# Staging the first MLP weight matrix in five slots instead of three, two of them in the x^T buffer

## The chip, the cores and the metric

One core of one Trainium2 chip runs the kernel. The metric is the device time of one execution in microseconds (us). TensorE, VectorE, ScalarE, GpSimd (POOL) and SyncE each run their own list of instructions in order and wait for one another through semaphores. DMA transfers are issued by SyncE, ScalarE or POOL.

## The reference

With x of 2048 rows (S) and 512 columns (D), the result mixes two branches by a gate per row, `out = g * a + (1 - g) * b`:

```python
g = sigmoid((x * gate_w).sum(-1, keepdims=True))
# a: 32 heads of 16; row s looks at the 8 rows s, s-2, ..., s-14
a = softmax(q . k * 16**-0.5, over the 8 rows) . v  @ wo        # q, k, v = x @ wqkv
# b: an MLP over the rows (tokens), not over the columns
h = layernorm(x)
u = gelu(einsum("bsd,sf->bdf", h, w1) + b1)      # F = 1792
b = transpose(einsum("bdf,fs->bds", u, w2) + b2)
```

W1 is 2048 x 1792 and W2 is 1792 x 2048, both bf16, 7.3 MB each, so neither is held on the chip whole.

## The kernel before

**Stages.** All on-chip buffers are views of one array, `arena`. TensorE's work is one fixed chain of steps: transposes of the first four tiles of x, the projections to q, k and v (L645), the first MLP product `u^T = W1^T h` (L853, called ph2), the second MLP product (L880, ph3) with the attention's output projection added into the same bank (L889), and the final scaling to the output. VectorE computes the attention: products of q and shifted k, sums, softmax pieces, and products with shifted v. TensorE's two short steps called sum0 and sum1 (L709 and L714), one for each half of the rows, sum the products over a head's 16 columns. They stand in TensorE's order inside ph2: sum0 inside block 1, sum1 after block 11. sum0 also computes the gate from x^T, and is the last reader of x^T.

**ph2.** It has 14 blocks (`ft` = 0 to 13), each of 16 matmuls of 128x128 weights by 128x512 data, one per tile of 128 rows. Blocks 2j and 2j+1 use load `w1_j`, which brings 256 columns of W1: 1 MB, as 16 x 256 elements for each of 128 partitions. There are three slots, and load j goes to slot j % 3:

```python
w1ld[j] = load("w1_%d" % j, W1W[:, j % 3, :, :], ..., ["w1s%d" % (j % 3)], order=j < 3)   # L529
```

So load j + 3 may start when block 2j + 1 has read its slot (L866 and L867). After each block ScalarE applies gelu and writes `UT[ft]`.

**ph3.** It has 16 tiles of 128 output rows, each of 14 matmuls in two halves of 7. Tiles 2j and 2j+1 use load `w2_j` (0.9 MB). The eight W2 slots (`W2S`, L368) lie on buffers no longer in use: two on x^T, three on the W1 slots, two on x, one on softmax scratch. The first six half tiles go in the order (0,0) (1,0) (2,0) (0,1) (1,1) (2,1) (L908). The output projection of tile i (`wo`, 4 matmuls) follows tile i + 5 (`LAG`); those of the last six stand at the very end, the last in two halves. It reads the attention's result `OT[i // 2]`, which VectorE writes.

**What sets the order.** A planner in the kernel (`_Sched`) lists every operation with what it reads and writes under names such as `w1s0` or `xt1`, derives the dependencies, and orders each engine's list by estimated times. An operation that writes a name waits for the last writer and all readers of that name. `after=` fixes only an order of issue, without a wait. W1 and W2 are loaded by SyncE, in the order `w1_0`, `w1_1`, `w1_2`, `wo`, `w1_3` to `w1_6`, `w2_0` to `w2_7`. SyncE holds a load until its semaphores are reached, and all loads behind it with it. `w1_1` and all later loads also wait for one accumulating copy of the attention (`late_dep`). The name list `XTALL` (L367) stands for all of x^T. A load with `XTALL` among its writes waits for sum0, and a second such load waits for the first to land.

**Other DMA.** POOL issues four copies of the softmax weights per half (L782, 512 KB each, on-chip to on-chip), which spread each head's weights over its columns for VectorE; they start when that half's softmax is done. For units 3, 4 and 5 of the v products POOL also issues accumulating copies (L822) which VectorE waits for before its next additions.

Of the kernel before, what the change touches and what calls it, by code (L numbers as in the profile page):

```python
# [5 lines left out]
BF16 = mybir.dt.bfloat16  # L6
# [6 lines left out]
S = 2048  # L13
# [5 lines left out]
NST = S // 128  # L19
NFT = F // 128  # L20
# [260 lines left out]
class _Mem:  # L281
# [17 lines left out]
    def view(self, name, dtype, dims, extra=0, p0=0, np_=128):  # L299
        base = self.arena[:].bitcast(dtype)  # L300
        pst = base.ap[0][0]
        esz = mybir.dt.size(dtype)
        o = self.off[name]
        assert o % esz == 0
        return bass.AP(base.tensor, p0 * pst + o // esz + extra, [[pst, np_]] + [list(d) for d in dims])


def bass_gated_mix__sliding_local_dilated__mixer_token_mlp__prompt_kernel(nc, A_x, A_wqkv, A_wo, B_x, B_w1, B_b1, B_w2, B_b2, gate_w, out, dbg=None):
    with contextlib.ExitStack() as es:
# [35 lines left out]
        view = m.view  # L345
        ps = es.enter_context(nc.psum_tensor("ps", [128, 8, 512], FP32))
# [7 lines left out]
        w1v = B_w1.rearrange("(st p) f -> p st f", p=128)  # L354
# [3 lines left out]
        X = view("X", BF16, [(D, NST), (1, D)])  # L358
        XT = view("XT", BF16, [(S, 4), (1, S)])
        UT = view("UT", BF16, [(D, NFT), (1, D)])  # L360
        WQKV = view("WQKV", BF16, [(3 * D, 4), (1, 3 * D)])
        W1W = view("W1", BF16, [(NST * 256, 3), (256, NST), (1, 256)])

        def w2view(name, extra=0):
            return view(name, BF16, [(256, NFT), (1, 256)], extra=extra)

        XTALL = ["xt0_%d_%d" % (t, k_) for t in range(4) for k_ in range(2)] + ["xt1", "xt2", "xt3"]  # L367
        W2S = [w2view("XT"), w2view("XT", NFT * 256), w2view("W1", NST * 256), w2view("W1", 2 * NST * 256), w2view("W1"),  # L368
               w2view("X"), w2view("X", NFT * 256), w2view("S4")]
        W2ALIAS = [XTALL, XTALL, ["w1s1"], ["w1s2"], ["w1s0"],  # L370
                   ["x%d" % t for t in range(7)], ["x%d" % t for t in range(7, 14)], ["s4", "s2", "s1", "rs", "rb"]]
        assert 4 * UT_ * 4 + 2 * UT_ * 4 + 2 * UT_ * 4 + UT_ * 2 >= NFT * 256 * 2
        WO = view("WO", BF16, [(D, 4), (1, D)])
# [57 lines left out]
        def col(v_, i):  # L431
            return bass.AP(v_.tensor, v_.offset + i, [list(v_.ap[0]), [1, 1]])
# [14 lines left out]
        def act(o_, i_, f_, **kw):  # L447
            return lambda e: e.activation(out=o_, in_=i_, func=f_, **kw)  # L448
# [29 lines left out]
        w1ld = {}  # L478
        late_dep = [[]]

        def load(name, dst, src, nbytes, writes, transpose=False, queue="sp", issue=0.5, order=True, deps=(), after=()):
            ds = sch.dsem(name)

            def fn(e):
                if transpose:
                    return e.dma_start_transpose(dst, src)
                return e.dma_start(dst, src)
            op = sch.dma(queue, fn, nbytes, ds, issue=issue, writes=writes, deps=list(deps) + late_dep[0],
                         after=list(after) + ([last_ld[queue]] if order and queue in last_ld else []), name=name)
            if order:  # L490
                last_ld[queue] = op
            return op
# [33 lines left out]
        ld_w("wv", 2, 0, 4, "wv")  # L526

        def ld_w1(j):
            w1ld[j] = load("w1_%d" % j, W1W[:, j % 3, :, :], w1v[:, :, 256 * j:256 * j + 256], S * 256 * 2, ["w1s%d" % (j % 3)], order=j < 3)  # L529

        def ld_w2(j):
            w1ld[7 + j] = load("w2_%d" % j, W2S[j], w2v[:, :, 256 * j:256 * j + 256], F * 256 * 2, ["w2_%d" % j] + W2ALIAS[j], order=False,
                               after=[w1ld[6 + j]])

        ld_w1(0)

        def f_warm(n):
# [9 lines left out]
        def PE(fn, dur, reads, writes, name, prio=0):  # L547
            op = A("pe", fn, dur, reads=reads, writes=writes, after=([chain[0]] if chain[0] is not None else []), name=name, prio=prio)
            chain[0] = op
            return op  # L550
# [234 lines left out]

        late_dep[0] = [qkd[0, 1]]
        ld_w1(1)
        ld_w1(2)
        load("wo", WO, A_wo.rearrange("(p t) d -> p t d", p=128, t=4), D * D * 2, ["wo"])

        def f_te(e):
            ins = None
            for k_ in range(4):
                ins = e.transpose(out=psb(3)[:, 128 * k_:128 * k_ + 128], in_=EB[:, 128 * k_:128 * k_ + 128], identity=IDENT)  # L794
            return ins
# [53 lines left out]
        def f_ph2(ft, bank, half):  # L849
            def fn(e):  # L850
                ins = None
                for st in range(8 * half, 8 * half + 8):
                    ins = e.matmul(ps[:, bank, :], lhsT=W1W[:, (ft // 2) % 3, st, 128 * (ft % 2):128 * (ft % 2) + 128], rhs=X[:, st, :],  # L853
                                   start=(st == 0), stop=(st == NST - 1))
                return ins
            return fn

        MLPB = [1, 2, 0, 1, 2, 0, 3, 1, 2, 0, 3, 1, 2, 0]
        for ft in range(NFT):
            bank = MLPB[ft]  # L860
            for half in range(2):
                PE(f_ph2(ft, bank, half), 1.735, ["x%d" % t for t in range(8 * half, 8 * half + 8)] + ["w1s%d" % ((ft // 2) % 3)], ["b%d" % bank],
                   "ph2_%d_%d" % (ft, half))
            A("act", act(UT[:, ft, :], ps[:, bank, :], AF.Gelu_apprx_tanh, bias=col(B1C, ft)), 0.7,
              reads=["b%d" % bank, "b1c"], writes=["ut%d" % ft] + (["wq0", "wq1", "wk", "wv"] if ft == 0 else []), name="gel%d" % ft, table=GELU)
            if ft % 2 == 1 and ft // 2 + 3 <= 6:  # L866
                ld_w1(ft // 2 + 3)  # L867
        for j in range(8):
            ld_w2(j)

# [5 lines left out]
        def f_ph3(i, bank, half, c0=0, c1=D):  # L876
            def fn(e):
                ins = None
                for ft in range(7 * half, 7 * half + 7):
                    ins = e.matmul(ps[:, bank, 0:c1 - c0], lhsT=W2S[i // 2][:, ft, 128 * (i % 2):128 * (i % 2) + 128], rhs=UT[:, ft, c0:c1],  # L880
                                   start=(ft == 0), stop=False)
# [27 lines left out]
        for i, half in head + tuple((i, half) for i in range(3, L) for half in range(2)):  # L909
            bank = banks[i]  # L910
# [11 lines left out]
        for hf, (c0, c1) in enumerate(CH):  # L922
            bank = lastb[hf]
# [90 lines left out]
```

## Time and profile before

| | us |
|---|---|
| median of 7 executions | 168.41 |
| range of the 7 | 167.74 to 170.65 |
| profiled execution, whole | 170.33 |
| its span, first to last instruction | 168.6 |
| TensorE busy | 162.7 |
| VectorE busy | 150.9 |
| ScalarE busy | 75.3 |
| POOL busy | 13.7 |

All times inside the profile are counted from the first instruction of the span. The profile follows the work that ended last backwards from the end; that chain is TensorE for 88% of the span and a load of MLP weights for 10%. Line numbers name lines of the kernel; many VectorE operations carry the line of one helper (L445), and ScalarE's that of another (L448). All plain loads are issued at L487. A row of the timeline gives the start, the length, the engine (SPq is SyncE's queue), the line, the operation and its operands; brackets at the end give idle time before it and what ended that.

The SyncE loads of the MLP weights in the profiled execution, from the trace's DMA issues and landings:

| load | issued | landed |
|---|---|---|
| w1_1, w1_2 | 43.00, 43.41 | 49.06, 52.62 |
| w1_3 | 57.06 | 62.97 |
| w1_4 | 64.19 | 70.43 |
| w1_5 | 71.10 | 76.79 |
| w1_6 | 78.01 | 94.83 |
| w2_0 | 78.42 | 97.49 |
| w2_1 | 97.51 | 102.68 |
| w2_2 | 97.92 | 105.87 |
| w2_3 | 98.66 | 109.02 |
| w2_4 | 103.75 | 112.18 |
| w2_5 | 105.38 | 115.34 |
| w2_6 | 108.51 | 118.48 |
| w2_7 | 115.29 | 127.85 |

### The profile page before, as it was taken

To read this page: it belongs to the slowest core of one execution; us is meant where nothing else is said; L and a number is where in the kernel's file an instruction comes from. 1 tells how busy PE (TensorE), PEld (TensorE's weight loads), DVE (VectorE), ACT (ScalarE), POOL (GpSimd) and SP (SyncE) were. 2 spreads that over 40 slices of the span, in tenths; PEclk is the share of its full clock that TensorE was granted. 3 is DMA by queue.
4 is the path that set the end of the run, shared out by engine and by line. 5 is a ranking of instruction groups with operands and counts; after the bars stand their busy time and mean duration, and the time that the engine had idled before them with its cause. 6 is when DMAs were issued, how large, how long until landed. Compare 5 with 4: busy or idle time off the path is not lost.

```text
span 168.6 us, 2019 instructions
## 1 busy us (share of the span) xinstructions
PE 162.7 (96%) x817; PEld 79.1 (47%) x817; DVE 150.9 (89%) x126; ACT 75.3 (45%) x104; POOL 13.7 (8%) x38
## 2 busy tenths in 40 slices
PE   7999999999999999999999499999999999999993
PEld 3765555555544444444443144444444444444752
DVE  1399999999999999999999992999999999999931
ACT  3256676666771899571112419500012221111154
POOL 7000002020000000004000000005000222000000
PEclk9999999999999999999999789999999999999999
DMA  5999999639496084588997759999995699971014
GB/s 158 331 153 267 225 306 184 124 58 189 134 298 198 18 235 111 138 239 113 180 259 213 211 171 291 290 290 291 320 246 179 142 215 190 207 170 52 31 51 135
DMA packets 44120, 32.11 MB, mean 190 GB/s; under 512 B 7248, under 2 KB 41680, under 8 KB 44112
## 3 DMA queue, kind: packets, MB, share of 16 engines
q1 hardware_dynamic: 40800, 21.96, 49.6%
q0 software_dynamic: 2608, 9.45, 28.1%
q10 hardware_dynamic: 704, 0.59, 1.1%
q8 instruction: 6, 0.10, 0.2%
q14 instruction: 2, 0.02, 0.0%
HBM read 18.88 MB, written 2.10 MB: 124 GB/s over the span
## 4 chain that ended last, share of the span: by engine, by line
PE 88%; DMA 10%; DVE 0%; issue 0%; POOL 0%; POOLq 0%
PE ps L880 29%; PE ps L645 23%; PE ps L853 22%; DMA arena<-in_B_w_dram 10%; PE ps L889 8%; PE ps L586 3%; PE ps L541 1%; PE ps L567 1%; PE ps L709 1%; PE ps L714 1%; PE ps L558 0%; DVE arena L929 0%; PE ps L794 0%; POOL arena L454 0%; PE ps L658 0%
## 5 line engine op out<-in xcount | busy, mean ns | idle before, releaser
L445 DVE TENSOR_TENSOR arena<-arena 128x4096 bf16<-128x4096 bf16 (+8 forms) x79 | 131.9, 1718 | 4.1 <-ACT arena L448 3.1
L853 PE MATMUL ps<-arena 128*128 128x512 bf16 x224 | 50.7, 388 | 2.2 <-DMA arena<-in_B_w_dram 2.2
L880 PE MATMUL ps<-arena 128*128 128x512 bf16 (+1 forms) x238 | 50.2, 366 | 0.0
L448 ACT ACTIVATE arena<-ps,arena 128x512 bf16<-128x512 f32 (+1 forms) x30 | 21.7, 728 | 63.3 <-PE ps L889 41.5
L448 ACT ACTIVATE arena<-ps 128x512 bf16<-128x512 f32 (+3 forms) x53 | 32.9, 629 | 19.2 <-PE ps L645 11.1
L645 PE MATMUL ps<-arena 128*128 128x512 bf16 x176 | 38.3, 379 | 0.0
L853 PEld LDWEIGHTS ps<-arena 128*128 128x128 bf16 x224 | 22.2, 100 | 30.0 <-ACT arena L448 2.7
L880 PEld LDWEIGHTS ps<-arena 128*128 128x128 bf16 x238 | 23.3, 98 | 25.3
L645 PEld LDWEIGHTS ps<-arena 128*128 128x128 bf16 x176 | 19.8, 113 | 17.7 <-ACT arena L448 0.3
L889 PE MATMUL ps<-arena 128*128 128x512 bf16 (+1 forms) x68 | 15.6, 366 | 0.0
L949 ACT ACT_TABLE_LOAD x11 | 14.1, 1283 | 2.5 <-issue 2.3
L782 POOL DMA_DIRECT2D arena<-arena x8 | 4.3, 561 | 77.1 <-DVE arena L445 77.1
L684 DVE BATCH_NORM_STATS2 arena<-arena 128x6 f32<-128x512 bf16 x16 | 9.9, 679 | 0.2 <-DMA arena<-in_A_x_dram 0.2
L889 PEld LDWEIGHTS ps<-arena 128*128 128x128 bf16 x68 | 6.7, 98 | 7.2
L448 ACT ACTIVATE arena<-arena 128x16 f32<-128x16 f32 (+5 forms) x10 | 6.8, 679 | 6.1 <-DVE arena L445 5.9
L579 DVE COPY arena<-ps 128x256 bf16<-128x256 bf16 x4 | 1.1, 291 | 5.1 <-PE ps L567 5.1
L698 DVE TENSOR_SCALAR arena<-arena 128x512 bf16<-128x512 bf16 x16 | 5.4, 413 | 0.0
L822 POOL DMA_DIRECT2D arena<-arena x3 | 3.6, 1200 | 19.0 <-DVE arena L445 19.0
L739 POOL DMA_DIRECT2D arena<-arena x2 | 2.5, 1234 | 29.7 <-DVE arena L695 21.1
L586 PE MATMUL ps<-arena 128*128 128x256 bf16 x32 | 4.6, 302 | 0.0
L929 DVE TENSOR_SCALAR arena<-ps,arena 128x256 bf16<-128x256 f32 x1 | 0.5, 543 | 4.4 <-PE ps L889 4.4
L586 PEld LDWEIGHTS ps<-arena 128*128 128x128 bf16 x32 | 3.5, 121 | 1.1 <-DVE arena L579 0.6
(39 smaller groups left out, 20.5 us busy)
## 6 DMA issues: line engine op xcount, KB each, us to landing
arena<-in_B_w_dram SPq DMA_DIRECT2D x7, 1024.0 KB, 6.2
arena<-in_B_w_dram SPq DMA_DIRECT2D x8, 896.0 KB, 10.0
arena<-arena POOLq DMA_DIRECT2D x5, 1024.0 KB, 8.2
arena<-arena POOLq DMA_DIRECT2D x8, 512.0 KB, 11.0
out_dram<-arena SPq DMA_DIRECT2D x15, 128.0 KB, 1.8
arena<-in_A_x_dram SPq DMA_DIRECT2D x3, 512.0 KB, 4.9
arena<-in_A_wqkv_dram SPq DMA_DIRECT2D x2, 512.0 KB, 5.1
arena<-in_A_wo_dram SPq DMA_DIRECT2D x1, 512.0 KB, 9.1
```

What stands on the lines that cost most here:

```text
L445: return lambda e: e.tensor_tensor(out=o_, in0=a_, in1=b_, op=op_)
L448: return lambda e: e.activation(out=o_, in_=i_, func=f_, **kw)
L586: ins = e.matmul(ps[:, dl, hb * 256:hb * 256 + 256], lhsT=sub(WQKV, dt * 3 * D + dl, [(4, 128)]), rhs=XT[:, dt, hb * 256:hb * 256 + 256], ...
L645: ins = e.matmul(ps[:, bank, :], lhsT=sub(WQKV, dt * 3 * D + tn * D + dl, [(4, 128)]), rhs=XT[:, dt, sb * 512:(sb + 1) * 512], start=(dt = ...
L684: A("dve", (lambda t_: lambda e: e.bn_stats(out=ST6[:, t_, :], in_=X[:, t_, :]))(t), 0.67, reads=["x%d" % t], writes=["st%d" % t], name="s ...
L698: A("dve", (lambda t_: lambda e: e.tensor_scalar(out=X[:, t_, :], in0=X[:, t_, :], scalar1=col(RSTD, t_), scalar2=col(NMR, t_), op0=ALU.mu ...
L782: prev = sch.dma("pool", (lambda d_, s_: lambda e: e.dma_start(d_, s_))(dst, src), 524288, sch.dsem("av%d_%d" % (h, c)), issue=1.0, reads= ...
L822: sch.dma("pool", (lambda o_, i_: lambda e: e.dma_start(o_, i_, accum_op=ALU.add, max_dma_last_dim=4096))(pw(0, 4), pw(4, 4)), 1800000, sc ...
L853: ins = e.matmul(ps[:, bank, :], lhsT=W1W[:, (ft // 2) % 3, st, 128 * (ft % 2):128 * (ft % 2) + 128], rhs=X[:, st, :], start=(st == 0), st ...
L880: ins = e.matmul(ps[:, bank, 0:c1 - c0], lhsT=W2S[i // 2][:, ft, 128 * (i % 2):128 * (i % 2) + 128], rhs=UT[:, ft, c0:c1], start=(ft == 0) ...
L889: ins = e.matmul(ps[:, bank, 0:c1 - c0], lhsT=OT[:, i // 2, dl, 128 * (i % 2):128 * (i % 2) + 128], rhs=WO[:, dl, c0:c1], start=False, sto ...
L949: e.preload_act_table_set(want)
```

## The change

The two halves of the x^T buffer (16 KB per partition in all, 8 KB each, the size of one W1 slot) become two more slots for W1 loads. `W1H[j]` and `W1R[j]` name the view and the slot of load j: slots 0, 1, 2, then x^T's halves, then slots 0 and 1 again. Load j + 5, not j + 3, follows block 2j + 1. Loads 3 and 4 are listed right after the load of `wo` and write all of `XTALL`, so load 3 waits for sum0, and load 4 waits for load 3 to land. Loads 4, 5 and 6 are issued in order. The first five W2 slots are assigned to the five W1 slots in the order in which those come free.

In the built program every engine has the same instructions in the same order as before. What differs is what SyncE's loads of W1 and W2 wait for, and where they put the data.

```diff
-        W1W = view("W1", BF16, [(NST * 256, 3), (256, NST), (1, 256)])
+        W1N = NST * 256
+        W1H = [view(n_, BF16, [(256, NST), (1, 256)], extra=k_ * W1N)
+               for n_, k_ in (("W1", 0), ("W1", 1), ("W1", 2), ("XT", 0), ("XT", 1), ("W1", 0), ("W1", 1))]
+        W1R = ["w1s0", "w1s1", "w1s2", "w1x0", "w1x1", "w1s0", "w1s1"]
...
-        W2S = [w2view("XT"), w2view("XT", NFT * 256), w2view("W1", NST * 256), w2view("W1", 2 * NST * 256), w2view("W1"),
+        W2S = [w2view("W1", 2 * W1N), w2view("XT"), w2view("XT", W1N), w2view("W1"), w2view("W1", W1N),
                w2view("X"), w2view("X", NFT * 256), w2view("S4")]
-        W2ALIAS = [XTALL, XTALL, ["w1s1"], ["w1s2"], ["w1s0"],
+        W2ALIAS = [["w1s2"], ["w1x0"], ["w1x1"], ["w1s0"], ["w1s1"],
                    ["x%d" % t for t in range(7)], ["x%d" % t for t in range(7, 14)], ["s4", "s2", "s1", "rs", "rb"]]
...
         def ld_w1(j):
-            w1ld[j] = load("w1_%d" % j, W1W[:, j % 3, :, :], w1v[:, :, 256 * j:256 * j + 256], S * 256 * 2, ["w1s%d" % (j % 3)], order=j < 3)
+            w1ld[j] = load("w1_%d" % j, W1H[j], w1v[:, :, 256 * j:256 * j + 256], S * 256 * 2, [W1R[j]] + (XTALL if j in (3, 4) else []), order=j < 3,
+                           after=[w1ld[j - 1]] if j > 3 else [])
...
         load("wo", WO, A_wo.rearrange("(p t) d -> p t d", p=128, t=4), D * D * 2, ["wo"])
+        ld_w1(3)
+        ld_w1(4)
...
-                    ins = e.matmul(ps[:, bank, :], lhsT=W1W[:, (ft // 2) % 3, st, 128 * (ft % 2):128 * (ft % 2) + 128], rhs=X[:, st, :],
+                    ins = e.matmul(ps[:, bank, :], lhsT=W1H[ft // 2][:, st, 128 * (ft % 2):128 * (ft % 2) + 128], rhs=X[:, st, :],
...
-            if ft % 2 == 1 and ft // 2 + 3 <= 6:
-                ld_w1(ft // 2 + 3)
+            if ft % 2 == 1 and ft // 2 + 5 <= 6:
+                ld_w1(ft // 2 + 5)
```

More of the change, by code (lines that the diff above doesn't have):

```diff
@@ L861, in bass_gated_mix__sliding_local_dilated__mixer_token_mlp__prompt_kernel @@
             for half in range(2):
-                PE(f_ph2(ft, bank, half), 1.735, ["x%d" % t for t in range(8 * half, 8 * half + 8)] + ["w1s%d" % ((ft // 2) % 3)], ["b%d" % bank],
+                PE(f_ph2(ft, bank, half), 1.735, ["x%d" % t for t in range(8 * half, 8 * half + 8)] + [W1R[ft // 2]], ["b%d" % bank],
                    "ph2_%d_%d" % (ft, half))
```

## The prediction

> **What bounds the kernel now.** I read the share of each engine first, then the chain that ended last, then the one gap in it, then the loads behind that gap. The head of the page:
>
> ```profile
> PE 162.7 (96%) x817; PEld 79.1 (47%) x817; DVE 150.9 (89%) x126; ACT 75.3 (45%) x104; POOL 13.7 (8%) x38
> ```
>
> TensorE is the bound, with VectorE close behind, so a gain for TensorE must be tested against VectorE. The chain that ended last, in order of time (start, length, what), shows where TensorE did not run:
>
> ```profile
> 62.44 15.55 PE ps L853 x72
> 77.99 0.02 issue
> 78.01 16.82 DMA arena<-in_B_w_dram
> 94.83 0.14 issue
> 94.97 8.75 PE ps L853 x32
> 103.72 18.13 PE ps L880 x84
> ```
>
> The 16.82 us of DMA are the life of one load, w1_6, from issue to landing, mostly beside matmuls. The loss is smaller. The last work before the gap is the second logit sum; it ends at 91.72 + 1.05 = 92.77. The next matmul, the first of block 12, starts at 94.97: 2.20 us of idle. From 9.91 us to the end this is the only break in TensorE's part of the chain. The timeline and the clock:
>
> ```profile
> 91.72 1.05 PE L714 MATMUL ps<-arena 128*32 128x512 bf16 x16
> 94.97 8.75 PE L853 MATMUL ps<-arena 128*128 128x512 bf16 x32 [2.20 <-DMA arena<-in_B_w_dram]
> ```
>
> ```profile
> 95.13:98.55 3.42, 3.42 (x9) 1.22 (x8) 3.32 (x5) 0.00 (x0) 0.00 (x0) 0.50 0.13 39
> 98.55:101.90 3.35, 3.35 (x17) 1.54 (x16) 2.56 (x2) 1.58 (x2) 0.00 (x0) 1.00 0.98 279
> ```
>
> In these windows (stretch, busy time of each engine, granted clock, DMA share, GB/s) the clock is 0.50 for 3.42 us after the gap. So 32 matmuls take 8.75 us where the row above, 72 in 15.55, gives 0.216 each: 6.91 us. The half clock costs 8.75 - 6.91 = 1.84 us. The whole loss is 2.20 + 1.84 = 4.04 us.
>
> Why was w1_6 late? SyncE's load issues, then the landing of the one at 78.0, then the four POOL copies of the attention weights:
>
> ```profile
> 64.19 0.37 SPq L487 DMA_DIRECT2D arena<-in_B_w_dram  x1
> 71.10 0.37 SPq L487 DMA_DIRECT2D arena<-in_B_w_dram  x1
> 78.01 12.88 SPq L487 DMA_DIRECT2D arena<-in_B_w_dram  x2
> ```
>
> ```profile
> L487 SPq DMA_DIRECT2D arena<-in_B_w_dram x1: 368/368/368, 78.0 to 78.0; - x1
> DMA to landing us min/median/max: 16.8/16.8/16.8
> ```
>
> ```profile
> L782 POOL DMA_DIRECT2D arena<-arena x4: 548/564/595, 75.6 to 77.2; - x4
> DMA to landing us min/median/max: 7.2/11.0/14.8
> ```
>
> The same 1 MB loads issued at 57.06, 64.19 and 71.10 land in 5.9, 6.2 and 5.7 us. Only the one issued after the copies, which move from 75.6 to 92.1, takes 16.8.
>
> **What the Trainium skill says.** "DMA: Bandwidth & Descriptors", section "Queues, rings and completion order": each DMA engine goes round robin between the queue rows it has work for, a packet at a time. The trace agrees: SyncE's load and POOL's copies share the time, and 5.7 us becomes 16.8. "TensorE: Matmul & The Clock Gate", section "Part 1: The HAM clock gate": the clock halves after an idle window of about 3.4 us, and the window is free-running. The stretch of 3.42 us at 0.50 agrees; an idle of 2.20 us was enough here, with narrow matmuls before it. Since the phase is free, another execution with the same gap may keep full speed. "SBUF — State Buffer", section "SBUF: two separate sides": DMA traffic and engines don't contend. The trace agrees: the 145 matmuls of L853 recorded between 59.7 and 91.0 us all have 379 ns, while the DMA share goes from 0.55 to 0.88.
>
> **The change, part by part.** Every engine keeps its instructions and their order; only the waits of SyncE's loads differ, so the price of issuing is that of before and only times move.
>
> *w1_3 and w1_4 into x^T.* x^T is last read by the first logit sum, which ends at 54.34 + 0.86 = 55.20. So w1_3 goes from 57.06 to 55.2 and lands at about 55.2 + 5.9 = 61.1 (needed by block 6 at 71.1). w1_4 lists all of x^T too and so waits until w1_3 has landed: the added wait. It issues at 61.1 instead of 64.19 and lands near 67.3 (needed at 78.0: 10.7 us of room). Queued behind that wait on SyncE are w1_5, w1_6 and all W2 loads.
>
> *w1_5 and w1_6.* Their slots are free after block 1 (57.1) and block 3 (64.2). w1_5 issues at about 61.5 instead of 71.10, w1_6 at 64.2 instead of 78.01. Back to back, 1 MB takes about 3.6 us at the 290 GB/s that the trace shows from 104 us on, so from w1_4's landing at 67.3: w1_5 at 71, w1_6 at 74.5. w1_6 is needed at 92.77. All W1 is in before the copies start at 75.6. The gap goes: -2.20, and with it the half clock: -1.84.
>
> *The W2 loads.* w2_0 takes slot 2, free after block 5: 71.1 instead of 78.42. w2_1, w2_2, w2_3 follow blocks 7, 9, 11: 78.0, 84.9 and 91.8, where they issued at 97.51, 97.92 and 98.66. w2_4, w2_5 and w2_6 still follow the end of the first MLP product. Now w2_1 is what meets the copies. Even with the 19.1 us that w2_0 took there it lands at 97.1; it is needed by the third half tile of the second product, at about 99.7 + 3.0 = 102.7. Cost nothing, with 5.6 us of cover; beyond it, one for one. The four copies feed VectorE's products, of which the first starts at 90.62 and its copy landed at 82.83: 7.8 us of cover.
>
> *VectorE.* TensorE comes 4.04 us earlier to the output projections, which need VectorE's attention. The end of VectorE's work and TensorE's last projections:
>
> ```profile
> 159.57 1.95 DVE L445 TENSOR_TENSOR arena<-arena 128x2048 bf16<-128x2048 bf16 x2
> 160.57 5.35 PE L889 MATMUL ps<-arena 128*128 128x512 bf16 x28
> ```
>
> VectorE ends at 161.52; projection 14, the first to read that result, starts 16 matmuls into this row, at 164.02. Room: 2.50 us, less than 4.04. But VectorE comes forward too:
>
> ```profile
> 104.25 1.23 DVE L445 TENSOR_TENSOR arena<-arena 128x1024 f32<-128x1024 bf16 x1 [3.10 <-ACT arena L448]
> ```
>
> It waited 3.10 us for the second exponential, which on ScalarE stood behind the gelu of block 12 (100.30), the late block. With that gelu at 96.3 the exponential starts at about 98.3 (its input is ready at 97.7) and ends at 100.2, before VectorE is done with its other work at 101.1. So VectorE gains the whole 3.10, and the room is 2.50 - 4.04 + 3.10 = 1.56 us. Next in line: VectorE, then nothing else.
>
> *Sum.* The profiled execution took 170.33 (span 168.6 and 1.7 around it): 170.33 - 4.04 = 166.29. The median of the seven runs is 168.41, lower by 1.92. After 9.91 us all of the chain but this gap is matmuls at full pace, so the 1.92 lie in the gap and its half clock, in the first 10 us, or outside the span. I take the first: without the half clock (1.84) the profiled execution would be at 168.49, beside the median. Then the median loses only the 2.20 of idle: 168.41 - 2.20 = 166.21. Both ways give the same floor, and I take 166.2. The three longest executions (169.0 to 170.65) would be those with half clock, and the spread of 2.9 us should shrink.
>
> **The rivals.**
> *The whole loss is in the median too*, and the 1.92 lie in the start or outside the span: 168.41 - 4.04 = 164.4. For it: a profiled execution may carry time of its own. Against: then nothing named explains the spread. 0.18.
> *The gap in an execution of median time is short*, because the transfers run less hindered without a profile: with 0.9 us left of it, 167.5. It also stands for the change not doing what it says, though w1_6 would have to take 28 us to be late, against 19.1 for the longest load in the trace. 0.11.
> *Slower: the accumulating copies of POOL at L822 come late.* VectorE has 0.1 us of room for the first (landed 138.56, used at 138.69). Landing took:
>
> ```profile
> L822 POOL DMA_DIRECT2D arena<-arena x3: 1176/1207/1218, 130.4 to 139.1; - x3
> DMA to landing us min/median/max: 8.2/9.8/12.8
> ```
>
> If earlier stores and loads push the first to the 14.8 us of the slowest weight copy, VectorE loses 14.8 - 8.2 - 0.1 = 6.5 us; 1.56 are free, so the end moves 4.9 later than forecast: 171.1. It costs from 1.56 us of delay on, and loses to before (by the median) from 1.56 + 2.2. Against: the loads end earlier, so copies meet less traffic. 0.05.
>
> **How the numbers follow.** Forecast 0.66, own range 165.4 to 166.9. About 1% (1.7 us, so 166.7) is what a measurement can tell from no change. Faster by over 1%: 0.62 of the forecast's 0.66 and the 0.18 of the first rival, 0.80. Within 1%: 0.04 of the forecast, the short gap's 0.11 and 0.01 of the last, 0.16. Slower 0.04. The range, 164.1 to 167.3, takes in the forecast, most of the first rival and the near part of the second.
>
> **What would show it.** Right: no idle of TensorE at L853 before block 12, clock 1.00 from warm-up to the end, w1_6 issued near 64 and landed before 76, W2 loads issued near 71, 78, 85 and 92, VectorE's 3.10 us wait gone, a span near 164.5. Wrong if TensorE waits at L880 for a load or at L889 for VectorE, or if the seven runs of before turn out to have the half clock in all of them.

## The result and the profile after

| | before | changed |
|---|---|---|
| median, us | 168.57 (58 executions) | 166.69 (23) |
| range, us | 167.07 to 172.49 | 165.86 to 167.62 |
| profiled execution, us | 170.33 | 166.81 |
| its span, us | 168.6 | 165.1 |

The ratio, changed over before, is 0.9904, with a 95% interval of 0.9887 to 0.9921: 1.6 us gained by the ratio, 1.9 by the medians. The ratio leaves out executions more than 1.5% above the fastest of their kernel, and those of before with the half clock (TensorE's clock at 0.50 after the gap) are among these, so it shows less than the medians. The forecast was 166.2, a gain of 2.2. The spread shrank from 5.4 us (58 executions) to 1.8 (23).

The chain of the changed kernel that ended last (start, length, what), in the stretch where a load stood before. L859 is the old L853. L718 is the old L714, which sums the logits of either half; L709, of the two lines given for sum0 and sum1, is the gate's part of sum0 alone.

```profile
62.64 0.22 PE ps L800 x4
62.86 29.35 PE ps L859 x136
92.22 0.98 PE ps L718 x16
93.19 7.01 PE ps L859 x32
100.21 18.13 PE ps L886 x84
```

From 62.86 on there is no load and no break. Block 12 (the first of the two in the row at 93.19) follows the second logit sum at once, and the 32 matmuls of blocks 12 and 13 take 7.01 us where they took 8.75. Between the two profiles the sum closes: 2.20 us of idle and 1.74 us of slower matmuls are gone, but this execution reached the end of the second logit sum 0.43 us later (93.20 against 92.77), and 2.20 + 1.74 - 0.43 = 3.51 us is what TensorE gained at the end of block 13. The half clock is gone (stretch, busy times, clock, DMA share, GB/s):

```profile
88.00:95.00 7.00, 7.00 (x45) 2.95 (x44) 7.00 (x3) 3.13 (x3) 0.00 (x0) 1.00 0.84 249
95.00:102.00 7.00, 7.00 (x35) 3.15 (x33) 6.84 (x8) 5.29 (x5) 0.00 (x0) 1.00 0.60 172
```

The loads, first w1_6, then w2_1 (line by line and with landing):

```profile
L490 SPq DMA_DIRECT2D arena<-in_B_w_dram x1: 3917/3917/3917, 64.6 to 64.6; - x1
DMA to landing us min/median/max: 11.4/11.4/11.4
...
L490 SPq DMA_DIRECT2D arena<-in_B_w_dram x1: 368/368/368, 78.4 to 78.4; - x1
DMA to landing us min/median/max: 16.6/16.6/16.6
```

w1_6 issues at 64.62 and lands at 76.05, 17 us before its use. That is 11.4 us from issue to landing, but w1_4 and w1_5 are queued ahead of it. The load that now meets POOL's weight copies (75.7 to 92.3) is w2_1, and it pays as w1_6 did: 16.6 us. But it lands at 95.0, and its first use is near 103. VectorE's 3.10 us wait at the second exponential is gone as well; its row now runs on:

```profile
97.81 4.68 DVE L448 TENSOR_TENSOR arena<-arena 128x4096 bf16<-128x4096 bf16 x3
```

### The profile page after: what moved, and what is told of

Same layout as the page of the kernel before. It is cut to its first block, busy times and chain, and to the rows that moved or that the text cites. A ratio compares the mean times of both kernels' runs of the same rounds, so it can differ in the third digit from the quotient of the medians.

```text
span 165.1 us, 2019 instructions
## 1 busy us (share of the span) xinstructions
PE 160.9 (97%) x817; PEld 78.7 (48%) x817; DVE 150.8 (91%) x126; ACT 75.3 (46%) x104; POOL 13.7 (8%) x38
## 4 chain that ended last, share of the span: by engine, by line
PE 95%; DMA 2%; DVE 0%; SPq 0%; issue 0%
PE ps L859 29%; PE ps L886 29%; PE ps L649 23%; PE ps L895 8%; PE ps L590 3%; DMA arena<-in_A_wqkv_dram 2%; PE ps L718 1%; PE ps L713 1%; DVE arena L935 0%; PE ps L571 0%; SPq L490 0%; PE ps L800 0%; PE ps L662 0%; PE ps L664 0%; PE ps L663 0%
## 5 line engine op out<-in xcount | busy, mean ns | idle before, releaser
L859 PE MATMUL ps<-arena 128*128 128x512 bf16 x224 | 49.0, 379 | 0.0
L649 PE MATMUL ps<-arena 128*128 128x512 bf16 x176 | 38.3, 379 | 0.0
L859 PEld LDWEIGHTS ps<-arena 128*128 128x128 bf16 x224 | 21.7, 98 | 26.6 <-issue 0.4
```

Source lines behind the costliest of these rows:

```text
L649: ins = e.matmul(ps[:, bank, :], lhsT=sub(WQKV, dt * 3 * D + tn * D + dl, [(4, 128)]), rhs=XT[:, dt, sb * 512:(sb + 1) * 512], start=(dt = ...
L859: ins = e.matmul(ps[:, bank, :], lhsT=W1H[ft // 2][:, st, 128 * (ft % 2):128 * (ft % 2) + 128], rhs=X[:, st, :], start=(st == 0), stop=(st ...
```

## The experiments

All ratios are to the kernel before, measured on the same chip: 67 executions with a median of 168.56 for the first four experiments, 44 with 168.28 for the others. A difference of some 0.3 us between medians of different experiments can thus be one of the series.

**Is the half clock in every execution?** The kernel before, unchanged.

> The kernel before, unchanged, for the clock and span of each of its executions. My theory: the half clock after the gap of TensorE is there in some executions only. Those with a mean clock of 1.00 lie between 167.3 and 168.8 us, those with 0.99 about 1.8 us above them (169 to 171), and the first kind are the majority. Rival: the half clock is in every execution (all at 0.99), and then the whole 4.04 us are in the median. Second rival: both kinds differ in nothing and the spread comes from the start of the span.

Of 67 executions of before on this chip, 61 have a mean clock of 1.00 (0.998 and up) and a median of 168.51; 6 have 0.99, all between 170.39 and 172.0, median 170.68. This experiment's own 14, with a median of 169.48, have 4 with 0.99 or less, all from 170.71 up. So the half clock is in a minority, some 2.2 us above the rest, and the median doesn't contain it. One part missed: executions at full clock reach 170.5, well above the 168.8 that I wrote, so some of the spread is not the half clock. The profile of this run has a gap of 2.69 us and the half clock after it:

```profile
95.44 4.87 PE L853 MATMUL ps<-arena 128*128 128x512 bf16 x14 [2.69 <-DMA arena<-in_B_w_dram]
```

```profile
95.40:99.70 4.30, 4.26 (x13) 1.62 (x14) 4.20 (x5) 0.00 (x0) 0.00 (x0) 0.61 0.17 49
```

**Idle and half clock apart.** Matmuls that nobody uses fill the gap of before:

```diff
+            if ft == 12:
+                def f_gap(e):
+                    ins = None
+                    for _ in range(8):
+                        ins = e.matmul(ps[:, 3, :], lhsT=ONES, rhs=ONES4, start=True, stop=True)
+                    return ins
+                PE(f_gap, 0.01, ["ones"], ["b3"], "gapfill").order.add(sums[1])   # sums[1]: the second logit sum
```

> The kernel before with 8 matmuls of 128x512 more (constants, into a bank that is free there, 8 x 0.216 = 1.73 us) between the second logit sum and block 12; they compute nothing that is used. TensorE then idles 0.5 us instead of 2.2 before block 12, but block 12 still starts when w1_6 lands. My theory: the clock is 1.00 in every execution, the executions over 169.5 us are gone, and the lowest and the median stay (lowest about 167.3, median 168.0 to 168.4), because the idle itself is still paid. Rival, half clock in every execution of before: the median falls by 1.8 us to about 166.7. If the idle is shorter than 1.73 us in some executions, those get slower by the difference.

The clock is 1.00 in all 22 executions, the longest is 169.48, the lowest 167.90, the median 168.71; ratio 1.0009 (0.9987 to 1.003). The median is 0.3 us and the lowest 0.6 us above what I wrote, the rest as expected. The timeline, with the filler at L866:

```profile
92.59 1.90 PE L866 MATMUL ps<-arena 128*128 128x512 bf16 x8
94.83 7.08 PE L854 MATMUL ps<-arena 128*128 128x512 bf16 x32 [0.34 <-DMA arena<-in_B_w_dram]
```

Block 12 still starts at 94.83, when w1_6 lands, and runs at full pace (7.08). A filled gap saves the half clock and nothing of the wait, and the median stays: the half clock is no part of it. The runs of all experiments agree on the cause of the half clock. Of the executions of kernels with the gap before block 12, 17 of 147 have a mean clock of 0.99 or less (6 of 67 and 4 of 44 of before, 4 of 14 in the first experiment, 3 of 22 in the third); of the 124 executions of the kernels without it, none.

**Only w1_6 late again.** The changed kernel, with w1_6 (and with it the W2 loads, which SyncE issues behind it) after block 7:

```diff
-                           after=[w1ld[j - 1]] if j > 3 else [])
+                           deps=[ph2_last] if j == 6 else [], after=[w1ld[j - 1]] if j > 3 else [])
...
-            if ft % 2 == 1 and ft // 2 + 5 <= 6:
-                ld_w1(ft // 2 + 5)
+            if ft == 1:
+                ld_w1(5)
+            if ft == 7:
+                ld_w1(6)
```

Here `ph2_last` is the latest block step.

> The changed kernel with one wait put back: w1_6 is issued only after block 7, as before, and w2_0, which follows it, with it. Five slots, and the earlier w1_4 and w1_5, stay. My theory, that the time of w1_6 against POOL's weight copies is all: it is issued near 78.4, lands near 95, TensorE idles about 2 us before block 12, and the time is that of before within 0.5 us (ratio 0.997 to 1.003). Rival, that the gain comes from the earlier w1_4, w1_5 or W2 loads: the time stays that of the changed kernel (ratio about 0.990).

Median 168.62, ratio 0.9997 (0.9968 to 1.0026): the gain is gone, and 3 of the 22 executions have the half clock again.

```profile
94.86 7.07 PE L859 MATMUL ps<-arena 128*128 128x512 bf16 x32 [2.01 <-ACT arena L451]
```

```profile
L490 SPq DMA_DIRECT2D arena<-in_B_w_dram x1: 367/367/367, 78.1 to 78.1; - x1
DMA to landing us min/median/max: 16.6/16.6/16.6
```

w1_6 issued at 78.09, landed at 94.73, and TensorE idled 2.01 us. The profile names ScalarE as the releaser because a copy there happens to end at 94.79. It is not the cause: in the changed kernel the same copy (93.25, 1.88 us) ended after block 12 had begun at 93.13. In this execution the clock stayed full after the 2.01 us, and the time (168.53) is the median's: here the idle alone is the loss. The changed kernel and this one differ in the W2 loads too, but TensorE waits for none of them, and the last experiment holds them back alone.

**Only the copies out of the way.** The kernel before, with three slots and old issue times; the second to fourth weight copies of the first half wait for w1_6:

```diff
+        for op in av0:                       # the three copies
+            op.deps.add(w1ld[6])
+            op.start = max(op.start, w1ld[6].start + 1e-3)
         sch.plan_waits()
```

> The kernel before, with three slots and the old issue times, but the second to fourth of POOL's first four weight copies wait until w1_6 has landed; the first goes as before. Their readers on VectorE come at 104 us and later. My theory, that the copies in flight make w1_6 late: w1_6, issued at 78.0, lands by 88 instead of 94.83, TensorE doesn't idle before block 12, the clock is 1.00, and the time is that of the changed kernel (ratio 0.988 to 0.993). Rival, that a load issued at 78 is too late or slow for its own reasons: w1_6 lands after 92.8 all the same and the time stays at that of before.

```profile
L487 SPq DMA_DIRECT2D arena<-in_B_w_dram x1: 368/368/368, 77.5 to 77.5; - x1
DMA to landing us min/median/max: 8.8/8.8/8.8
```

```profile
92.24 7.08 PE L856 MATMUL ps<-arena 128*128 128x512 bf16 x32
99.16 3.19 PE L883 MATMUL ps<-arena 128*128 128x512 bf16 x14
104.30 1.90 PE L883 MATMUL ps<-arena 128*128 128x512 bf16 x8 [1.96 <-DMA arena<-in_B_w_dram]
```

Half right. Issued at the same time, w1_6 took 8.8 us instead of 16.8 and landed at 86.4; the gap before block 12 is closed, so the copies are what made it late. (In both kernels w2_0 is queued right behind it.) But the median is 167.97, ratio 0.9977 (0.9955 to 0.9999), not 0.990. The copies, now later, meet w2_1, which with three slots can't issue before 89.1 (it waits for w2_0 on x^T). It takes 15.1 us, and TensorE idles 1.96 us at the second product instead. The collision has moved to the next load without room.

**Half of the change.** Four slots; the other half of x^T takes w2_0:

```diff
-               for n_, k_ in (("W1", 0), ("W1", 1), ("W1", 2), ("XT", 0), ("XT", 1), ("W1", 0), ("W1", 1))]
+               for n_, k_ in (("W1", 0), ("W1", 1), ("W1", 2), ("XT", 0), ("W1", 0), ("W1", 1), ("W1", 2))]
...
-        ld_w1(4)
...
-            if ft % 2 == 1 and ft // 2 + 5 <= 6:
-                ld_w1(ft // 2 + 5)
+            if ft % 2 == 1 and ft // 2 + 4 <= 6:
+                ld_w1(ft // 2 + 4)
```

(`W1R`, `W2S` and `W2ALIAS` follow.)

> Half of the change: four W1 slots (one half of x^T joins), loads issued one block pair sooner, w1_6 after block 5. The other half of x^T takes w2_0. My theory: w1_6 is issued near 71.2 and lands near 77 to 79, ahead of most of the weight copies; TensorE doesn't idle before block 12, and the time is that of the changed kernel (ratio to before 0.988 to 0.993). Rival, that the fifth slot is needed because the copies still slow a load of that time: w1_6 lands after 92.8 and the time is that of before.

Median 166.39, ratio 0.9881 (0.9847 to 0.9916): all of the gain. TensorE waits for no load of MLP weights.

```profile
L490 SPq DMA_DIRECT2D arena<-in_B_w_dram x1: 368/368/368, 70.9 to 70.9; - x1
DMA to landing us min/median/max: 6.1/6.1/6.1
```

w1_6, 7 us earlier than before, lands at 77.0, 1.4 us after the first of the copies was issued. One slot more is enough; the two kernels can't be told apart by these runs.

**How much room VectorE has.** The changed kernel with its last v product done in part or wholly twice:

```diff
+            if u == 7:
+                AV(tt(pv[:, 0:4], sub(V5, PAD + 256 * u, [(-2, 4), (VR, 4), (1, UT_)]), sub(AVW[h], c * NW * UT_, [(UT_, 4), (0, 4), (1, UT_)]), ALU.mult), 0.01,
+                   reads=["avw%d_%d" % (h, c)] + vr + ["vpad"], writes=res, name="avx")   # second run: 8 in place of 4
             AV(tt(pv, sub(V5, PAD + 256 * u, ...
```

> The changed kernel with half of VectorE's last v product done twice (one more 128x4096 multiplication, about 2.2 us, ahead of that product; the result is the same). In the profile of the changed kernel VectorE's attention ends at 158.54 and projection 14 starts at 160.51: 1.97 us of room. My theory: 2.2 us cost 0.2 us, the time is 166.7 to 167.1, about that of the changed kernel. Rival, that VectorE bounds the changed kernel already: 168.9.

> The same with the whole of that product done twice (one more 128x8192 multiplication, about 4.3 us). My theory: 4.3 - 1.97 = 2.4 us are paid, 169.1 us, and TensorE waits for VectorE at the output projections of the end. Rival, that the work beside it hides it too: 166.7.

The first: median 166.91, ratio 0.9935 (0.9907 to 0.9963), 0.2 us above the median of the changed kernel. The second: 169.38, ratio 1.0082 (1.0059 to 1.0106), 2.7 us above. Their timelines of TensorE show where, the first run's and then the second's:

```profile
160.29 1.91 PE L898 MATMUL ps<-arena 128*128 128x512 bf16 x11 [0.48 <-DVE arena L448]
```

```profile
158.89 3.63 PE L898 MATMUL ps<-arena 128*128 128x512 bf16 x16 [1.65 <-DVE arena L448]
163.08 1.91 PE L898 MATMUL ps<-arena 128*128 128x512 bf16 x11 [0.56 <-DVE arena L448]
```

By the medians 2.2 us is hidden but for 0.2; of 4.3 us about 1.6 are hidden and the rest is paid at the output projections. The profiles can be compared without their starts, from the end of the second logit sum to the end of the span: the two runs then take 0.7 and 2.5 us longer than the changed kernel, so that 1.6 and 1.8 us were hidden. Either way VectorE is next in line, with room between about 1.6 and 2.0 us.

**Do the earlier W2 loads matter?** The changed kernel with w2_0 held until block 11:

```diff
-["w2_%d" % j] + W2ALIAS[j], order=False,
+["w2_%d" % j] + W2ALIAS[j], order=False, deps=[ph2_op[11]] if j == 0 else [],
```

Here `ph2_op[11]` is the last step of block 11.

> The changed kernel with the W2 loads held back: w2_0 is issued only after block 11 (about 92), and the others after it. The W1 loads stay early. My theory, that the earlier W2 loads neither gain nor cost: w2_0 lands by 98, w2_1 by 102, both before they are needed (100.2 and 103.2), and the time is that of the changed kernel (ratio to before 0.988 to 0.993). Rival, that a part of the gain lies in the earlier W2 loads: TensorE waits at the second product, 0.5 us or more lost.

Median 167.03, ratio 0.9926 (0.9895 to 0.9956). The interval overlaps that of the changed kernel, so the median alone settles nothing. The profile shows a cost, though not where either theory looked. No load was late: w2_0 landed at 98.6, w2_1 at 101.6. VectorE, then TensorE:

```profile
137.82 22.84 DVE L448 TENSOR_TENSOR arena<-arena 128x2048 bf16<-128x2048 bf16 x14 [3.06 <-DMA arena<-arena]
```

```profile
156.53 3.63 PE L896 MATMUL ps<-arena 128*128 128x512 bf16 x16 [0.34 <-DVE arena L448]
160.72 1.91 PE L896 MATMUL ps<-arena 128*128 128x512 bf16 x11 [0.56 <-DVE arena L448]
```

The W2 loads end later. w2_7 takes 20.1 us to land (131.4) and is still on its way when the first accumulating copy is issued (126.4); the copy takes 11.4 us instead of 8.0 (landed at 137.80). The other profiles fit: this copy took 7.8 to 8.2 us in the seven with no W2 load beside it, and 9.1 and 10.9 us in the two with one (the second and the fourth experiment). VectorE waits 3.06 us for the copy; after the room is used up, TensorE waits 0.34 + 0.56 = 0.90 us. From the end of the second logit sum on, this execution takes 1.2 us more than the changed kernel's; an earlier start (92.17 against 93.20) hides that in its time.

## Why the prediction was right, point by point

- **The bound, and the gap of w1_6 as the only loss:** right. The gap comes back when w1_6 is issued late again (the third experiment), and one extra slot removes it.
- **Why w1_6 was late:** right. With three of the four copies out of its way it takes 8.8 us instead of 16.8.
- **The half clock, left out of the median:** right, and the step that decided the number. The rival of 164.4, with the whole 4.04 us in the median, falls by the first two experiments. One of my two reasons for it was wrong, though. I gave the three longest of the seven executions (169.0 to 170.65) to the half clock; in the later series it begins only at 170.39, so at most one of them had it. The conclusion held without that support. What lifts the executions between 169 and 170.4 was not isolated; the start can give 1 us of it, for the second logit sum ends anywhere between 92.17 and 93.22 in the ten profiles.
- **Its size, 1.84 us:** 1.74. I took 6.91 us for the 32 matmuls at full clock, from the mean of the row above; in the changed kernel they take 7.01.
- **The idle, 2.20 us:** right for the profiles, mis-sized for the median. From the end of the second logit sum to the end of the span, the two profiles with a late w1_6 and a full clock (the third and the second experiment) take 2.1 and 2.2 us more than the changed kernel. The median gained less: the executions of before at full clock lie 1.8 us above the changed kernel (168.51 in the first experiment's series, against 166.69), and by the ratio the gain is 1.6. Profiles with the gap left open show an idle of 2.01, 2.20 and 2.69 us. How long an execution idles that isn't profiled is not on record, so it stays open whether the missing 0.3 to 0.6 us are a shorter idle or a difference in the starts.
- **Faster by over 1%, 0.80:** the ratio says 0.96%, the medians 1.1%. The result sits on the bound, and the 2.2 us that I forecast would have cleared it.
- **Times of the loads:** w1_4 landed at 68.80 (67.3 forecast), w1_5 at 72.44 (71), w1_6 at 76.05 (74.5), w2_1 at 95.02 (97.1 at the latest). The 3.6 us between the landings of loads in a row was right. The 1.5 us too early come before w1_4's landing: w1_3 was issued 0.5 us later than forecast, and w1_4 took 7.3 us, not 6.2. The wait that was added for w1_4 cost nothing.
- **TensorE's pace beside DMA traffic:** right, but the 379 ns of each recorded matmul don't show it: matmuls start 216 ns apart, so these lengths overlap and are no pace. The pace does show it: 136 matmuls in 29.35 us of the changed kernel, across the copies, and 72 in 15.55 us of before, most of them ahead of the copies, are 0.216 us each.
- **VectorE's room, 1.56 us:** 1.97 in the profile, since TensorE came only 3.51 us earlier and VectorE 2.98; 1.6 to 2.0 by the doubled product.
- **The W2 moves at no cost:** right for TensorE's loads, but the step was too short. It asked only whether loads come in time. In the profile of the last experiment a W2 load that ends late overlaps the first accumulating copy, which takes 3.4 us longer; in the two other profiles with such an overlap it is slower too. So the earlier loads also keep the way free for these copies. That is the mechanism of my slower rival, at 3.06 us of VectorE's time; in the changed kernel w2_7 had landed (121.1) before the first copy was issued (127.4).

## What to carry to other kernels

Ask of a late load what else moves at that time, and move the load ahead of it, not merely earlier: 7 us were as good as 13 here because both issue it before the copies. When one transfer is freed from a collision, look for the next one that meets it, and give that one room: w2_1, which now takes the hit, has 8 us to spare, and where it had none (the fourth experiment) TensorE waited 1.96 us for it. And before a loss in one profile is credited to the median, ask which part of it every execution pays.

## What the runs showed of the hardware

- A 1 MB load through SyncE's queue took 5.7 to 6.2 us with little or nothing beside it (w1_3 to w1_5 of before). With a 0.9 MB load queued behind it, it took 8.8 us beside one 512 KB on-chip copy (the fourth experiment), and 16.6 to 17.3 us beside four (the four profiles with w1_6 issued late and the copies left as they were).
- TensorE's clock was halved for about 3.4 us after an idle of 2.20 us (before) and of 2.69 us (the first experiment), and stayed full after 2.01 us (the third) and 1.96 us (the fourth). The mean clock of 0.99 or less that goes with this was in 17 of 147 executions with the gap before block 12, and in none of the 22 in which eight unused matmuls filled that gap. Two profiles of each kind don't give a bound.
